# Talking-heads attention and a feed-forward block: the second batch's second mixing by three float16 products

## The chip, the cores and the metric

One core of a Trainium2 chip. The metric is device time in microseconds (us). Engines named here: TensorE (PE, with its weight loads as PEld), VectorE (DVE), ScalarE (ACT), GpSimd (POOL) and SyncE (SP), whose queue issues all DMAs.

## The reference

```
scores = einsum('bhij,hg->bgij', (q @ k^T) / 8, w_pre)       # first mixing, over 12 heads
attn   = exp(scores - max); attn = attn / (sum(attn) + 1e-9)
attn   = einsum('bhij,hg->bgij', attn, w_post)               # second mixing
x      = (attn @ v), as (1792 tokens, 768)
h = x @ w_in;  g = h * sigmoid(1.702 h);  out = g @ w_out    # 768 -> 2048 -> 768
```

There are 4 batches of 12 heads, 448 rows and 64 columns; everything comes in and goes out as float32.

## The kernel before

**Steps.** A batch's attention is done in 45 steps of 10 rows of the sequence (the last has 8). In a step the 10 rows and 12 heads are 120 partitions, and the 448 columns lie along the free axis, so that mixing the heads is one matrix product with a 120x120 matrix (`KG` = 120). There are 180 steps in all, numbered by `i`; steps 45 to 89 are the second batch (`b` = 1).

A step goes: `gather` (a DMA brings the scores `r`), `mix` (PE, first mixing into PSUM `mx`), `peak` (DVE, the row maximum), `expo` (ACT, the exponential `e` and its sum), `shifted` (POOL) and `inverse` (DVE), which make the factor `rs` of the normalization, and then the second mixing into PSUM `pp`, in one of two ways:

- **float32** (`whole`): `weigh_mix` (POOL) multiplies the 120x120 mixing matrix `wp` by `rs`, and `post_whole` (PE) multiplies the exponentials `e` with it: four chunks of 112 columns, one float32 product each, which the trace shows as two matmul instructions. `keep_whole` (ACT) copies `pp` to SBUF as one float32 array `p`.
- **float16**: `weigh` (POOL) makes `w` = `e` times `rs` in float32; `upper` (ACT) makes the same rounded to float16, `a1`; `lower` (POOL) subtracts the two to get the rest, `a2`, in float16. `post` (PE) adds three float16 products for each of the four chunks: `a1` with both parts of the mixing matrix (`wp1`, `wp2`) and `a2` with `wp1`. `keep_upper` (ACT) and `keep_lower` (DVE) store `pp` as two float16 parts.

The product of q and k (`scores`) and that with v (`context`) have the same two kinds: one float32 product, or three float16 products of two-part operands. In the kernel before, `WHOLE = 2` decides all of it: batches 0 and 1 go in float32, batches 2 and 3 by parts.

**Feed-forward.** The weights come as 32-bit halves of 64-bit numbers and are converted on the chip, in 16 conversions (8 slices of `w_in` and of `w_out`) of three parts each. A part takes on DVE `magnitude` (L473), `least` (L477), `shift` (L481), `rest` (L487), `sign` (L493) and, later, `w_lower` (L526), and on ACT a sum of squares and `w_upper`. The converted slices go to DRAM (`wd`) and come back as `wt` for each of 32 units (8 slices for each of 4 batches). A unit is 36 matmuls for h (`hidden`, L557), tanh and gating on ACT and DVE, and 36 matmuls for the output (`project`, L595).

**The order of the work.** The order on each engine is worked out when the program is built, by a greedy planner: `add` enters a task with its engines, an assumed duration, the tasks it comes after, a due time counted in steps and the buffers that it takes, and `run_all` picks among those that can start within 0.1 us the one that is due first. On the chip each engine then goes through its own list in that order. Conversions become due every 7 steps, then every 5, and their loads wait for the exponential of a given step (`gated_by`); the feed-forward's units follow at 12 pieces of work per 5.6 steps. The planner may put some copies and sums on either ACT or DVE. Buffers that matter here: `e` and `w` share three, `a1` and `wr` share three, `a2` has three, `mx` and `pp` have two PSUM banks each, and three banks serve the scores' products and the feed-forward.

Of the kernel before, what the change touches and what calls it, by code (L numbers as in the profile page):

```python
# [18 lines left out]

B, H, S, D = 4, 12, 448, 64  # L20
WHOLE = 2
DM, DFF = 768, 2048
NT = B * S
GI = 10
GPB = -(-S // GI)
GPC = 12
# [13 lines left out]
def attention_then_feed_forward(ctx, tc, q, k, v, w_pre, w_post, w_in, w_out, out):  # L40
    nc = tc.nc
# [14 lines left out]
    steps = [(b, g) for b in range(B) for g in range(GPB)]  # L56
# [9 lines left out]
    ex = keep.tile([128, B], F32, name="ex")  # L66
# [12 lines left out]
    def root_bits(e, m):  # L79

        nc.vector.tensor_scalar_max(m, m, 1e-30)
        nc.vector.tensor_scalar(
            e.bitcast(I32), m.bitcast(I32), 1, 0x7F800000,
            op0=ALU.logical_shift_right, op1=ALU.bitwise_and,
        )
# [55 lines left out]
    def top_of(name, b):  # L141
        i = 3 * b + "kqv".index(name)
        return tops[:, i:i + 1]

    def scale(name, b):

        m = top_of(name, b)
        e = stat.tile([128, 1], F32, name=f"e{name}_{b}", tag="e" + name)
        s = stat.tile([128, 1], F32, name=f"s_{name}{b}", tag="s" + name)
        root_bits(e, m)  # L150
        nc.vector.reciprocal(s, e)
        nc.vector.tensor_scalar_mul(s, s, 2.0 ** -50)
        nc.vector.tensor_scalar_mul(e, e, 2.0 ** 63)
        st["e" + name, b], st["s" + name, b] = e, s
        if name == "v":
            nc.vector.tensor_scalar(
                ex[:, b:b + 1], e, e_wp, 2.0 ** -12, op0=ALU.mult, op1=ALU.mult
            )
            if b < WHOLE:
                xs = st["xs", b] = keep.tile([128, 1], F32, name=f"xs_{b}")  # L160
                nc.vector.reciprocal(xs, ex[:, b:b + 1])

    def mixing(b):
        wa = keep.tile([KG, KG], F32, name=f"wa_{b}", tag="wa", bufs=2)
# [51 lines left out]
    def scores(b, c, pr, tag=("gen", 3)):  # L216
# [3 lines left out]
        w = NPAIR // THIRDS  # L220
        if b < WHOLE:
            qf, kf = st["q", b, pr // w], st["k", b, pr // w]
# [30 lines left out]
    def rows_of(g):  # L253
        return g * GI, min(GI, S - g * GI)
# [11 lines left out]
    def mix(i):  # L266
        b, g = steps[i]
        K = rows_of(g)[1] * H
        mx = ps.tile([128, 512], F32, name=f"mx_{i}", tag="mx", bufs=2)[:KG]
        row["mx", i] = mx  # L270
        nc.tensor.matmul(  # L271
            mx[:K, :S], st["wa", b][:K, :K], row.pop(("r", i))[:K, :], start=True, stop=True
        )

    def peak(i):
        K = rows_of(steps[i][1])[1] * H
        nm = stat.tile([KG, 1], F32, name=f"nm_{i}", tag="nm")
        nc.vector.tensor_reduce(nm[:K], row["mx", i][:K, :S], axis=AX.X, op=ALU.max, negate=True)  # L278
        row["nm", i] = nm

    def expo(i):
        K = rows_of(steps[i][1])[1] * H
        e = flow.tile([KG, S], F32, name=f"e_{i}", tag="e", bufs=3)
        sm = stat.tile([KG, 1], F32, name=f"sm_{i}", tag="sm")
        nc.scalar.activation(  # L285
            e[:K], row.pop(("mx", i))[:K, :S], AF.Exp, bias=row.pop(("nm", i))[:K, 0:1],
            scale=1.0, accum_out=sm[:K, 0:1],
        )
        row["e", i], row["sm", i] = e, sm

    def shifted(i):
        K = rows_of(steps[i][1])[1] * H
        sm = row.pop(("sm", i))
        rs = stat.tile([KG, 1], F32, name=f"rs_{i}", tag="rs")
        by = 1.0 if steps[i][0] < WHOLE else 2.0 ** -10
        nc.gpsimd.tensor_scalar(rs[:K], sm[:K], 1e-9, by, op0=ALU.add, op1=ALU.mult)  # L296
        row["rs", i] = rs

    def inverse(i):
        K = rows_of(steps[i][1])[1] * H  # L300
        nc.vector.reciprocal(row["rs", i][:K], row["rs", i][:K])  # L301
# [57 lines left out]
    def mixed_to(i):  # L359
        b, g = steps[i]  # L360
        n = rows_of(g)[1]
        c, off = g // GPC, (g % GPC) * GI
        if off == 0:
            shape, kind = ([CP, NR, H, CI], F32) if b < WHOLE else ([CP, 2, NR, H, CI], F16)
            st["p", b, c] = mixed.tile(shape, kind, name=f"p_{b}_{c}", tag="p")
        p = st["p", b, c]
        if b < WHOLE:
            return p.rearrange("p r h i -> p (r h) i")[:, :, off:off + n]
        return p.rearrange("p t r h i -> p t (r h) i")[:, :, :, off:off + n]
# [4 lines left out]
    def keep_upper(i):  # L374
        p = row["p", i] = mixed_to(i)
        nc.scalar.copy(p[:, 0], row["pp", i])  # L376

    def keep_lower(i):
        p = row.pop(("p", i))
        nc.vector.tensor_tensor(p[:, 1], row.pop(("pp", i)), p[:, 0], op=ALU.subtract)  # L380


    def context(b, c, pr):
# [5 lines left out]
        w = H // THIRDS  # L389
        if b < WHOLE:  # L390
            for jc in range(NR):
# [247 lines left out]
    def add(eng, occ, f, after=(), due=0.0, lat=None, size=0.0, takes=(), kind="", bias=0.0, behind=None):  # L639

        occ = occ if isinstance(occ, dict) else {e: occ for e in eng.split("/")}
        if lat is None:
            lat = {e: o + (0.2 if e == "PE" else 0.1) for e, o in occ.items()}
        lat = lat if isinstance(lat, dict) else {e: lat for e in occ}
        j = {"eng": tuple(occ), "occ": occ, "lat": lat, "f": f, "due": due, "size": size, "takes": list(takes),
             "kind": kind, "bias": bias, "left": 0, "then": [], "next": [], "at": None, "from": 0.0}
        for a in after:
            if a is not None:
                a["then"].append(j)
                j["left"] += 1  # L650
        if behind is not None:
            behind["next"].append(j)
            j["left"] += 1
        for x in j["takes"]:
            x[1].append(j)
        if not j["left"]:
            waiting.append(j)
        return j
# [207 lines left out]
    def step_tasks(i):  # L866

        b, g = steps[i]
        c, whole = g // GPC, b < WHOLE
        takes_p = [("p", p_home[b, c])] if g % GPC == 0 else []  # L870
        mx, pp = [], []
        m = mixes[i] = add("PE", 0.755, lambda: mix(i), [gathers.get(i), mixes.get(i - 1), mixers.get(b)], i - 1,
                           takes=[("mx", mx)])
        r_home[i].append(m)
        k = add("D", 0.53, lambda: peak(i), [m], i - 1, 0.62)
        early = expos.get(i, {"then": []})["then"]
        e = expos[i] = add("A", 0.62, lambda: expo(i), [k, expos.get(i - 1)], i - 0.8, 0.73, takes=[("e", e_home[i])])
        e["then"] += early
        mx += [k, e]
        r = add("G", 0.28, lambda: shifted(i), [e], i - 0.5, 0.26)  # L880
        v = add("D", 0.08, lambda: inverse(i), [r], i - 0.5, 0.16)

        def emit_post():
            (post_whole if whole else post)(i)
            last_pp_home.append(pp)

        if whole:
            wr = []
            w = add("G", 0.45, lambda: weigh_mix(i), [v], i, 0.4, takes=[("a1", wr)])
            p = add("PE", 0.84, emit_post, [w, e, posts.get(i - 1)], i + 1, takes=[("pp", pp)])  # L890
            wr.append(p)
            e_home[i].append(p)
            q = add("A", 0.45, lambda: keep_whole(i), [p], i + 2, 0.58, takes=takes_p)
            pp.append(q)
        else:
            w_home, a1, a2 = [], [], []
            w = add("G", 0.72, lambda: weigh(i), [v], i, 0.7, takes=[("e", w_home)])
            u = add("A", 0.56, lambda: upper(i), [v], i + 0.3, 0.66, takes=[("a1", a1)])
            lo = add("G", 1.12, lambda: lower(i), [w, u], i + 0.6, 1.05, takes=[("a2", a2)])
            e_home[i] += [w, u]  # L900
            w_home.append(lo)
            p = add("PE", 0.64, emit_post, [lo, u, posts.get(i - 1)], i + 2, takes=[("pp", pp)])
            a1 += [lo, p]
            a2.append(p)
            h = add("A", 0.45, lambda: keep_upper(i), [p], i + 2.8, 0.56, takes=takes_p)
            q = add("D", 0.56, lambda: keep_lower(i), [h], i + 3.2, 0.65)
            pp += [h, q]
        posts[i], keeps[i] = p, q
        p_home[b, c].append(q)
        if not first_post:  # L910
            first_post.append(p)
# [138 lines left out]
    for i in range(N):  # L1050
        if i + AHEAD < N:
            b, g = steps[i + AHEAD]
# [24 lines left out]
        b, g = steps[i]  # L1077
# [18 lines left out]
    for u in range(NU):  # L1096
        s, b = units[u]
# [6 lines left out]
        for fc in range(SF):  # L1104
            gen, th = [], []
            j = None
            for x in range(3):
                due = due_of["h", u, fc, x] - 1.5 * (x > 0)
                j = add("PE", 1.134, lambda u=u, fc=fc, x=x: hidden(u, fc, x), [got[0, u], x_done[b], j], due,
                        takes=[] if x else [("gen", gen)], kind="ff")  # L1110
# [15 lines left out]
        for e in range(NCC):  # L1126
# [6 lines left out]
            takes = [("acc", acc_home[b])] if (s, e) == (0, 0) else [("pt", pt, "A")] if 0 < s < NS - 1 else []  # L1133
# [60 lines left out]
```

## Time and profile before

| | |
|---|---|
| median of 3 runs | 928.07 us (927.72 to 929.06) |
| the profiled execution's own time | 930.12 us |
| its span, first to last instruction | 928.4 us |
| matmul instructions | 6972 |
| busy over the span: PE, DVE, ACT, POOL | 97%, 63%, 64%, 36% |
| mean granted TensorE clock | 0.992 of full speed |

Busy time of an engine counts a moment once, even where two of its instructions overlap; TensorE's matmuls overlap in the trace, where their ends are modelled, so the rate of TensorE is read from start to start. The "chain of waits" follows the work that ended last back in time, at each step to what released it. A stretch is given in us from the start of the span.

### The profile page before, as it was taken

How to read it: one execution, taken by the hardware profiler on the slowest of the kernel's cores; microseconds unless marked ns; L12 is line 12 of the kernel's file. 1: busy time of each engine (PE TensorE's matmuls, PEld its weight loads, DVE VectorE, ACT ScalarE, POOL GpSimd, SP SyncE). 2: the span in 40 equal slices, each digit the busy share in tenths (PEclk: the TensorE clock that was granted, in tenths of full speed). 3: DMA queues.
4: the chain of work that ended last, by engine and by line, in shares of the span. 5: the costliest groups of instructions: out<-in, count | busy, mean ns of one | idle time of the engine just before them, and what ended most of it. 6: DMA issues, size and time to landing. Idle time of an engine off the chain costs nothing.

```text
span 928.4 us, 18998 instructions
## 1 busy us (share of the span) xinstructions
PE 897.2 (97%) x6972; PEld 535.5 (58%) x6972; DVE 589.4 (63%) x1342; ACT 593.3 (64%) x1328; POOL 337.8 (36%) x532
## 2 busy tenths in 40 slices
PE   7879989999999999989999999999999999999998
PEld 5455656656566566655656555555656666545554
DVE  2678787687789978977567656567555554332233
ACT  2668787697875776765696776666675665324342
POOL 0212222221225313546346744455344553203431
PEclk9999999999999999999999999999999999999999
DMA  7878999997988796669576575567443422343322
GB/s 235 288 257 298 321 305 329 320 314 230 335 294 287 231 299 207 204 194 328 168 249 221 162 238 162 164 176 255 140 154 111 129 99 83 123 133 132 136 75 88
DMA packets 66256, 196.76 MB, mean 212 GB/s; under 512 B 7699, under 2 KB 32403, under 8 KB 66163
## 3 DMA queue, kind: packets, MB, share of 16 engines
q1 hardware_dynamic: 66162, 195.54, 65.1%
q8 instruction: 55, 0.90, 0.4%
q14 instruction: 39, 0.31, 0.1%
HBM read 138.89 MB, written 56.62 MB: 211 GB/s over the span
## 4 chain that ended last, share of the span: by engine, by line
PE 75%; DVE 9%; DMA 6%; ACT 5%; issue 2%; POOL 2%; SPq 1%; ACTq 0%; POOLq 0%; DVEq 0%
PE po L595 20%; PE h L557 20%; PE mx L271 12%; PE pp L316 5%; PE av L394 3%; PE av L405 3%; PE qk L225 3%; PE qk L235 3%; DMA r<-sd 2%; PE pp L353 2%; PE pp L355 2%; PE pp L354 2%; DVE nm L278 2%; ACT e L285 1%; ACT waste L96 1%
## 5 line engine op out<-in xcount | busy, mean ns | idle before, releaser
L557 PE MATMUL h<-x,wt 128*128 128x448 f16 x1152 | 246.8, 352 | 3.2 <-DMA wt<-wd 2.9
L595 PE MATMUL po<-g,wt 128*128 128x448 f16 x1152 | 239.7, 352 | 4.3 <-DVE th L576 2.4
L271 PE MATMUL mx<-r,wa 120*120 120x448 f32 x360 | 172.3, 563 | 5.2 <-DMA r<-sd 3.1
L557 PEld LDWEIGHTS <-wt 128*128 128x128 f16 x1152 | 109.2, 98 | 115.5 <-issue 26.4
L285 ACT ACTIVATE e<-mx,nm 120x448 f32<-120x448 f32 x180 | 113.9, 633 | 96.4 <-DVE nm L278 84.5
L595 PEld LDWEIGHTS <-wt 128*128 128x128 f16 x1152 | 109.9, 98 | 108.4 <-issue 16.7
L296 POOL TENSOR_SCALAR rs<-sm 120x1 f32<-120x1 f32 x180 | 46.8, 260 | 336.6 <-ACT e L285 333.3
L278 DVE TENSOR_REDUCE nm<-mx 120x1 f32<-120x448 f32 x180 | 111.4, 619 | 46.3 <-PE mx L271 44.9
L623 POOL TENSOR_TENSOR acc<-acc,pt 128x448 f32<-128x448 f32 x64 | 72.8, 1138 | 117.3 <-ACT pt L617 116.9
L316 PEld LDWEIGHTS pp<-wr,e 120*112 120x112 f32 x720 | 84.4, 177 | 40.9 <-issue 18.9
L576 DVE SCALAR_TENSOR_TENSOR th<-th,h 128x448 f32<-128x448 f32 x64 | 39.6, 619 | 105.9 <-ACT th L572 105.5
L340 POOL TENSOR_TENSOR a<-w,a 120x448 f16<-120x448 f32 (+1 forms) x90 | 95.8, 1064 | 26.3 <-POOL w L326 17.6
L316 PE MATMUL pp<-wr,e 120*112 120x120 f32 x720 | 91.4, 270 | 6.0 <-POOL wr L306 6.0
L246 ACT COPY sc<-qk 120x448 f32<-120x448 f32 (+1 forms) x150 | 74.5, 532 | 15.7 <-PE qk L225 11.3
L619 DVE SCALAR_TENSOR_TENSOR acc<-po,ct,acc 128x448 f32<-128x448 f32 x104 | 70.3, 679 | 22.0 <-PE po L595 21.1
L271 PEld LDWEIGHTS mx<-r,wa 120*120 120x120 f32 x360 | 57.8, 184 | 37.4 <-issue 16.2
L326 POOL TENSOR_SCALAR w<-e,rs 120x448 f32<-120x448 f32 (+1 forms) x90 | 60.5, 672 | 40.8 <-DVE rs L301 35.0
L617 ACT ACTIVATE pt<-po,ct 128x448 f32<-128x448 f32 x64 | 40.6, 634 | 51.1 <-PE po L595 51.0
L334 ACT ACTIVATE a<-e,rs 120x448 f16<-120x448 f32 (+1 forms) x90 | 60.3, 670 | 18.4 <-DVE rs L301 17.2
L380 DVE TENSOR_TENSOR p<-pp,p 112x480 f16<-112x480 f32 (+1 forms) x90 | 58.4, 649 | 19.2 <-ACT p L376 18.9
L306 POOL TENSOR_SCALAR wr<-wp,rs 120x120 f32<-120x120 f32 (+1 forms) x90 | 47.4, 527 | 54.0 <-DVE rs L301 33.7
L353 PE MATMUL pp<-wp,a 120*112 120x120 f16 x360 | 62.3, 217 | 0.0
(123 smaller groups left out, 1323.0 us busy)
## 6 DMA issues: line engine op xcount, KB each, us to landing
wt<-wd SPq DMA_DIRECT2D x64, 768.0 KB
r<-sd SPq DMA_DIRECT2D x176, 210.0 KB
sd<-sc SPq DMA_DIRECT2D x66, 420.0 KB
w<-in_moe_w_in_dram SPq DMA_DIRECT2D x24, 512.0 KB
w<-in_moe_w_out_dram SPq DMA_DIRECT2D x24, 512.0 KB
wd<-w_p SPq DMA_DIRECT2D x16, 768.0 KB
sd<-sc SPq DMA_DIRECT2D x24, 308.0 KB
out_dram<-acc SPq DMA_DIRECT2D x24, 224.0 KB
```

The source lines that it names most:

```text
L246: (nc.scalar.copy if eng == "A" else nc.vector.tensor_copy)(t[:n, x, :], two[x][:n, :S])
L271: nc.tensor.matmul(mx[:K, :S], st["wa", b][:K, :K], row.pop(("r", i))[:K, :], start=True, stop=True)
L278: nc.vector.tensor_reduce(nm[:K], row["mx", i][:K, :S], axis=AX.X, op=ALU.max, negate=True)
L285: nc.scalar.activation(e[:K], row.pop(("mx", i))[:K, :S], AF.Exp, bias=row.pop(("nm", i))[:K, 0:1], scale=1.0, accum_out=sm[:K, 0:1],)
L316: nc.tensor.matmul(pp[:CP, jc * K:(jc + 1) * K], e[:K, jc * CP:(jc + 1) * CP], wr[:K, :, :n], start=True, stop=True,)
L326: nc.gpsimd.tensor_scalar(w[:K], e[:K], row["rs", i][:K, 0:1], 1.0, op0=ALU.mult, op1=ALU.mult)
L340: nc.gpsimd.tensor_tensor(a2[:K], row.pop(("w", i))[:K], row["a1", i][:K], op=ALU.subtract)
L353: nc.tensor.matmul(o, a1[:K, js], wp1[:K, :, :n], start=True, stop=False)
L557: nc.tensor.matmul(h, w[:, i, c, fc * 128:(fc + 1) * 128], x[:, j, c, :], start=(n == 0), stop=(n == len(terms) - 1),)
L595: nc.tensor.matmul(po, w[:, j, fc, e * 128:(e + 1) * 128], g[:, i, fc, :], start=(n == 0), stop=(n == len(terms) - 1),)
L619: nc.vector.scalar_tensor_tensor(a, po, c, a, op0=ALU.mult, op1=ALU.add)
L623: nc.gpsimd.tensor_tensor(a, a, st.pop(("pt", u, e)), op=ALU.add)
```

## The change

A second bound, `EXACT = 1`, decides about the second mixing; `WHOLE = 2` still decides about the products with k and with v. So batch 1 takes `weigh`, `upper`, `lower` and `post`, and then `keep_whole`: one float32 copy of `pp`, and the float32 product with v. The factor `rs` of batch 1 gets the 2^-10 of the float16 way, and the scale `xs` that the output of the attention is multiplied by follows from that.

```diff
+EXACT = 1
 ...
             if b < WHOLE:
                 xs = st["xs", b] = keep.tile([128, 1], F32, name=f"xs_{b}")
-                nc.vector.reciprocal(xs, ex[:, b:b + 1])
+                if b < EXACT:
+                    nc.vector.reciprocal(xs, ex[:, b:b + 1])
+                else:
+                    nc.vector.tensor_scalar_mul(xs, s, 2.0 ** -15)
 ...
-        by = 1.0 if steps[i][0] < WHOLE else 2.0 ** -10
+        by = 1.0 if steps[i][0] < EXACT else 2.0 ** -10
 ...
-        c, whole = g // GPC, b < WHOLE
+        c, whole = g // GPC, b < EXACT
 ...
-            h = add("A", 0.45, lambda: keep_upper(i), [p], i + 2.8, 0.56, takes=takes_p)
-            q = add("D", 0.56, lambda: keep_lower(i), [h], i + 3.2, 0.65)
-            pp += [h, q]
+            h = add("A", 0.45, lambda: (keep_whole if b < WHOLE else keep_upper)(i), [p], i + 2.8, 0.56, takes=takes_p)
+            q = h if b < WHOLE else add("D", 0.56, lambda: keep_lower(i), [h], i + 3.2, 0.65)
+            pp += [h] if b < WHOLE else [h, q]
```

## Rows read from the trace of the kernel before

**Rows 1.** The profile's page, busy time of each engine over the span.
```profile
span 928.4 us, 18998 instructions
PE 897.2 (97%) x6972; PEld 535.5 (58%) x6972; DVE 589.4 (63%) x1342; ACT 593.3 (64%) x1328; POOL 337.8 (36%) x532
```

**Rows 2.** The page's chain of work that ended last, by engine and by line.
```profile
PE 75%; DVE 9%; DMA 6%; ACT 5%; issue 2%; POOL 2%; SPq 1%; ACTq 0%; POOLq 0%; DVEq 0%
PE po L595 20%; PE h L557 20%; PE mx L271 12%; PE pp L316 5%; PE av L394 3%; PE av L405 3%; PE qk L225 3%; PE qk L235 3%; DMA r<-sd 2%; PE pp L353 2%; PE pp L355 2%; PE pp L354 2%; DVE nm L278 2%; ACT e L285 1%; ACT waste L96 1%
```

**Rows 3.** Stretches: length; busy us (instructions) per engine; granted clock, DMA share, GB/s.
```profile
160.00:365.00 205.00, 201.50 (x1392) 125.40 (x1393) 167.78 (x413) 150.72 (x364) 55.93 (x103) 0.99 0.86 281
180.00:200.00 20.00, 19.88 (x113) 11.80 (x112) 17.99 (x48) 18.11 (x47) 6.07 (x14) 1.00 1.01 308
280.00:320.00 40.00, 37.82 (x250) 23.46 (x249) 38.00 (x78) 24.86 (x57) 17.02 (x22) 1.00 0.78 255
365.00:412.00 47.00, 44.12 (x375) 26.56 (x372) 39.67 (x89) 31.73 (x71) 21.69 (x29) 1.00 0.66 206
425.00:765.00 340.00, 339.09 (x3123) 201.49 (x3122) 204.57 (x430) 230.54 (x502) 170.58 (x249) 1.00 0.58 182
```

**Rows 4.** Stretches of the float32 second mixing's matmuls alone (L316): PE, PEld.
```profile
160.00:368.00 208.00, 44.93 (x360) 42.84 (x360) 0.99 0.86 282
```

**Rows 5.** Timeline of PE, batch 1: start, duration, instructions.
```profile
263.14 0.92 PE L271 MATMUL mx<-r,wa 120*120 120x448 f32 x2
263.90 0.98 PE L316 MATMUL pp<-wr,e 120*112 120x120 f32 x8
264.72 1.30 PE L557 MATMUL h<-x,wt 128*128 128x448 f16 x6
```

**Rows 6.** Timeline of PE, batch 2: a step's first and last float16 product.
```profile
570.80 0.22 PE L353 MATMUL pp<-wp,a 120*112 120x120 f16 x1
...
571.38 0.22 PE L355 MATMUL pp<-wp,a 120*112 120x120 f16 x1
571.43 0.73 PE L557 MATMUL h<-x,wt 128*128 128x448 f16 x3
```

**Rows 7.** The page's groups: count, busy us, mean ns, idle before and its releaser.
```profile
L340 POOL TENSOR_TENSOR a<-w,a 120x448 f16<-120x448 f32 (+1 forms) x90 | 95.8, 1064 | 26.3 <-POOL w L326 17.6
L326 POOL TENSOR_SCALAR w<-e,rs 120x448 f32<-120x448 f32 (+1 forms) x90 | 60.5, 672 | 40.8 <-DVE rs L301 35.0
L334 ACT ACTIVATE a<-e,rs 120x448 f16<-120x448 f32 (+1 forms) x90 | 60.3, 670 | 18.4 <-DVE rs L301 17.2
L306 POOL TENSOR_SCALAR wr<-wp,rs 120x120 f32<-120x120 f32 (+1 forms) x90 | 47.4, 527 | 54.0 <-DVE rs L301 33.7
```

**Rows 8.** Groups on DVE in 160 to 365, three of the conversion's lines.
```profile
L487 DVE SCALAR_TENSOR_TENSOR w_f<-w,w_f 128x512 int32<-128x512 int32 x26 | 18.4, 707 | 0.4
L526 DVE SCALAR_TENSOR_TENSOR w_p<-w_f,w_s,w_p 128x512 f16<-128x512 f32 x24 | 17.3, 746 | 1.1 <-ACT w_p L521 0.9
L477 DVE TENSOR_SCALAR w_f<-w_f 128x512 f32<-128x512 f32 x26 | 11.7, 449 | 0.3
```

**Rows 9.** The same lines on DVE in 365 to 412.
```profile
L526 DVE SCALAR_TENSOR_TENSOR w_p<-w_f,w_s,w_p 128x512 f16<-128x512 f32 x6 | 5.1, 871 | 0.0
L487 DVE SCALAR_TENSOR_TENSOR w_f<-w,w_f 128x512 int32<-128x512 int32 x3 | 3.1, 1033 | 0.1
L477 DVE TENSOR_SCALAR w_f<-w_f 128x512 f32<-128x512 f32 x3 | 3.0, 1009 | 0.0
```

**Rows 10.** Timeline of all engines at 391 to 397.
```profile
391.43 1.08 POOL L340 TENSOR_TENSOR a<-w,a 120x448 f16<-120x448 f32 x1
...
391.66 1.40 DVE L487 SCALAR_TENSOR_TENSOR w_f<-w,w_f 128x512 int32<-128x512 int32 x1
...
397.05 0.74 PE L557 MATMUL h<-x,wt 128*128 128x448 f16 x3 [2.88 <-DMA wt<-wd]
```

## The prediction

> **What bounds the kernel now.** I read the page's busy times first, then its chain of waits, then a table of stretches, and last the timeline of single steps. The busy times say TensorE: 97% of the span, with DVE and ACT at 63% and 64% [rows 1]. The reader is to check that this isn't only a long tail of overlapping matmuls, and the chain of waits does that: 75% of the time that led to the end is PE's own work, and the float32 second mixing (L316) alone is 5% of it [rows 2]. But the mean hides the stage that matters. Batch 1's 45 second mixings, 8 matmul instructions each, lie between 160 and 368 us [rows 4], and in 160 to 365 DVE is busy 167.8 of 205 us (82%) and ACT 150.7 (74%), against 60% and 68% in 425 to 765 [rows 3]. The conversions of the weights run in that stage too, 26 parts of them [rows 8]. So TensorE is the bound there, at 201.5 of 205 us, but with two engines not far behind it.
>
> **What the change does on TensorE.** A float32 mixing starts at 263.90 and the next matmul at 264.72, that is 0.82 us a step [rows 5]. By three float16 products it is 12 matmuls from 570.80 to the next product at 571.43, 0.63 us [rows 6]; both are followed by the same kind of matmul. So 0.19 us goes from each step, times 45 is 8.55 us of TensorE's work, all of it in a stage where TensorE has 3.5 us of idle time in 205. Nothing else on TensorE changes: the products with k and v stay float32.
>
> **What it adds elsewhere.** ACT gets `upper`, 45 x 0.670 = 30.2 us [rows 7]; `keep_whole` stays. POOL loses `weigh_mix`, 45 x 0.527 = 23.7, and gets `weigh` and `lower`, 45 x (0.672 + 1.064) = 78.1 [rows 7], a net 54.4. DVE gets no instruction: `inverse` stays, `keep_lower` isn't used, and the scale `xs` is one small multiplication in place of one reciprocal, once in the program, which I cost at nothing because it lies in the work of sizing v, many steps before the first use. POOL goes from 55.9 to about 110 us of 205, which is the share that it has in 425 to 765 (170.6 of 340) with PE busy 339.1 of 340 [rows 3]: POOL by itself isn't the bound. ACT goes from 150.7 to about 181 us, or 90% of a stage of 201 us. No DMA is added or moved past another in its due time.
>
> The new path is also longer. In float32 the post waits for a POOL instruction of 0.527 us after the reciprocal; now it waits for 0.672 + 1.064 = 1.74 us of POOL, or 1.2 us more [rows 7]. The post becomes due one step later (i + 2 in place of i + 1), and a step of this stage takes 205/45 = 4.6 us, so I cost the latency at nothing: the feed-forward's matmuls and the next `mix` cover it. If that cover is gone, it costs 1.2 us at the four ends of a chunk where `context` waits for the last copy, 5 us in all, and that is within the range below. The buffers `e`, now shared with `w`, were shared in batches 2 and 3 already, at 340 us for 75 steps (4.5 us each), with PE idle for 0.9 us [rows 3].
>
> **What of the 8.55 us is left.** That depends on how much TensorE idles once ACT, DVE and POOL are fuller. The trace has no stretch with all three as full as they will be, so I bound the idle share by the nearest three [rows 3]. At 180 to 200, ACT is at 91% and DVE at 90%, and PE idles 0.12 of 20 us (0.6%). At 280 to 320, DVE is at 95%, and PE idles 2.18 of 40 (5.5%). At 365 to 412 the very mix of the changed kernel is seen, float16 steps beside conversions, and PE idles 2.88 of 47 (6.1%), which is one wait for a converted weight tile [rows 10]. TensorE's work in the stage becomes 201.5 - 8.55 = 192.95 us. At 0.6% idle the stage lasts 194.1 us (10.9 less than now), at 6.1% it lasts 205.5 (0.5 more). I take the mean of the three, 4.1%, since the first has the fullness and the last the mix: 192.95/0.959 = 201.2 us, 3.8 less than now. Before 160 and after 412 the work is unchanged, and from 425 to 765 TensorE idles for 0.9 us [rows 3], so that what is won is kept and what is lost isn't made up.
>
> The durations are from an execution of 930.12 us with a span of 928.4; it would come to 926.3. The median of the runs is 2.05 us below it, and so I forecast 928.07 - 3.8 = 924.3 us.
>
> **The rivals.**
>
> *Full gain (917.2 us).* The planner moves copies from ACT to DVE and back as they fill, and the idle share is that of 180 to 200: 10.9 us less. For it: the fullest stretch of the two engines has the least idle time [rows 3]. Against: it is only 20 us long.
>
> *VectorE becomes the bound (933 us, slower).* In 365 to 412, where POOL does float16 steps, the conversion's DVE instructions are longer than in 160 to 365, where it doesn't: L477 1009 ns against 449, L487 1033 against 707, L526 871 against 746 [rows 8, 9]. That is 0.560 + 0.326 + 0.125 = 1.01 us for each part of a conversion. The timeline shows how: L487, started 0.23 us after POOL's L340, takes 1.40 us in place of 0.7 and ends 0.55 us after it [rows 10], so it looks as if it had waited for POOL's instruction to end. The 26 parts of 160 to 365 would so cost DVE 26.3 us more, 194.1 in all. At the share that DVE reaches in its two fullest stretches, 95% and 90% [rows 3], 92.5% between them, the stage lasts 209.8 us, 4.8 more than now: 933 us (204 to 216 us of stage by the two shares, 927.4 to 938.8 us). It decides from the point where DVE at 90% needs more than 205 us, which is 16.7 us of added work or 0.64 us a part; the planner has no such cost and can't evade it. Against it: the means of L477 and L487 in 365 to 412 come from three instructions each.
> The Trainium skill (SBUF — State Buffer, section "Who interferes with whom") says that VectorE and GpSimd share one pair of ports under an exclusive lock: a VectorE instruction with two SBUF inputs, or in a two-port mode, and a GpSimd instruction that reads SBUF block each other for a whole instruction, whichever started first. By that rule L477, L487 and L526 would all be exposed, which the longer means agree with, and the time would be this rival's.
>
> *The wait for weights eats it (928 us).* At 394 TensorE waits 2.88 us for a converted tile [rows 10]. If the conversions don't come earlier, TensorE arrives up to 8.55 us sooner and waits that much longer. Against it: their loads are gated by the exponentials of given steps, which come earlier as well; DVE has to keep pace.
>
> *The change doesn't do what it says*: the float16 products being no faster. The 90 steps of batches 2 and 3 already have them, so I give it nothing.
>
> **How the numbers follow.** A measurement of this kernel can tell 0.2%, 1.9 us, from no change: 926.2 to 929.9 us. My forecast's case, 921 to 926.2, gets 0.41; full gain, below 921, gets 0.15; the wait for weights, within 0.2%, gets 0.17; VectorE as the bound, above 929.9, gets 0.27. So faster 0.56, same 0.17, slower 0.27. Cases of both signs hold much of the chance; the likeliest one's own range is 921 to 926.2. The range that should hold the time 8 times in 10 reaches from the full gain to just above the slower rival's 933: 917 to 935, which leaves out some 0.05 below and 0.13 above.
>
> **What would show it.** Right: batch 1's `pp` takes 12 matmuls in 0.63 us; ACT's 30 us and POOL's 54 us are added between 160 and 360; the last second mixing of batch 1 starts about 4 us earlier and everything after it by as much; PE's idle time in the stage rises from 3.5 to about 8 us. Wrong towards slower: L477, L487 and L526 in that stage near their 365 to 412 means, DVE over 90%, and PE waiting for DVE or for `wt`. Wrong towards faster: PE's idle time no larger than now. What would make it wrong altogether is another order of work after 412 that leaves TensorE idle where it now isn't, since the planner works the whole order out anew.

## The result and the profile after

The changed kernel takes 941.20 us (median of 6 runs, 938.96 to 945.77) against 929.32 us for the kernel before (6 runs, 927.72 to 930.67): a ratio of 1.0130, with a 95% interval of 1.0102 to 1.0158. It is slower, where 3.8 us less were forecast. The ratios, here and below, are taken against runs of the kernel before that were measured beside each kernel; they differ from the quotient of the two medians by up to 0.2%. The profiled execution has a span of 940.2 us.

The page of the changed kernel, busy times and the chain of waits (its lines are numbered 4 higher from the step functions on; L316 is now L320, L353 to L355 are L357 to L359):

```profile
span 940.2 us, 19441 instructions
PE 893.8 (95%) x7152; PEld 527.5 (56%) x7152; DVE 615.0 (65%) x1345; ACT 615.6 (65%) x1369; POOL 405.3 (43%) x582
PE 56%; DVE 15%; ACT 2%; DMA 1%; issue 1%; POOL 1%; SPq 0%; ACTq 0%; POOLq 0%
```

Against [rows 1] PE is busy 3.4 us less in a span that is 11.8 us longer, and DVE, to which the change itself gives no instruction (the planner moved three there), is busy 25.6 us more. The chain's shares add up to 77% here (it couldn't be followed back further) and to 100% in [rows 2], so that PE's fall from 75% to 56% says little by itself; but DVE's share rises from 9% to 15% in spite of it. In 220 to 430, which both chains cover, DVE has 43 of the 210 us before and 121 after, PE 119 and 46, POOL 7 and 6. The stretches, with the columns of [rows 3], say where:

```profile
160.00:375.00 215.00, 195.59 (x1544) 115.53 (x1546) 189.78 (x411) 168.68 (x398) 118.76 (x148) 0.98 0.81 264
280.00:320.00 40.00, 32.06 (x243) 18.95 (x241) 39.61 (x64) 24.67 (x54) 29.42 (x30) 0.91 0.75 243
430.00:780.00 350.00, 349.63 (x3257) 208.64 (x3257) 214.35 (x444) 239.88 (x519) 179.18 (x257) 1.00 0.59 184
```

All of it is in batch 1's stage: from the first mixing of step 45 to that of step 110, 294.6 us became 307.0, and the 12.4 us are lost before step 90. In 160 to 375 TensorE idles 215 - 195.6 = 19.4 us (9.0%), against 3.5 of 205 before [rows 3]; from 430 to 780 it idles 0.4 us, so it is busy there as it was. The float16 mixing itself does what it should, 12 matmuls from 186.95 to 187.58, 0.63 us (timeline of PE):

```profile
186.95 0.22 PE L357 MATMUL pp<-wp,a 120*112 120x120 f16 x1
...
187.53 0.22 PE L359 MATMUL pp<-wp,a 120*112 120x120 f16 x1
187.58 0.97 PE L275 MATMUL mx<-r,wa 120*120 120x448 f32 x2
```

DVE's groups in 160 to 376 show the conversion's six lines. Where the same line is in [rows 8], the mean was 707 (now L491), 746 (L530) and 449 ns (L481). The other three before (now L497, L477 and L485), in 160 to 365, and then all six after:

```profile
L493 DVE SCALAR_TENSOR_TENSOR w_f<-w,w_f 128x512 int32<-128x512 int32 x25 | 19.1, 764 | 0.2
L473 DVE TENSOR_SCALAR w_f<-w 128x512 int32<-128x512 int32 x26 | 11.3, 433 | 3.2 <-DMA w<-in_moe_w_in_dram 2.3 <-DMA w<-in_moe_w_out_dram 0.8
L481 DVE TENSOR_SCALAR w_f<-w_f 128x512 int32<-128x512 int32 x26 | 11.0, 425 | 0.4
```

```profile
L491 DVE SCALAR_TENSOR_TENSOR w_f<-w,w_f 128x512 int32<-128x512 int32 x25 | 23.0, 923 | 0.2
L497 DVE SCALAR_TENSOR_TENSOR w_f<-w,w_f 128x512 int32<-128x512 int32 x25 | 20.3, 814 | 0.3
L530 DVE SCALAR_TENSOR_TENSOR w_p<-w_f,w_s,w_p 128x512 f16<-128x512 f32 x25 | 19.9, 820 | 0.5 <-ACT w_p L525 0.5
L485 DVE TENSOR_SCALAR w_f<-w_f 128x512 int32<-128x512 int32 x25 | 15.2, 611 | 0.3
L477 DVE TENSOR_SCALAR w_f<-w 128x512 int32<-128x512 int32 x26 | 14.4, 553 | 0.5 <-DMA w<-in_moe_w_in_dram 0.5
L481 DVE TENSOR_SCALAR w_f<-w_f 128x512 f32<-128x512 f32 x25 | 13.5, 544 | 0.3
```

The timeline of all engines at the largest wait shows how a longer DVE instruction becomes idle time of TensorE:

```profile
307.65 1.38 POOL L627 TENSOR_TENSOR acc<-acc,pt 128x448 f32<-128x448 f32 x1
308.08 1.24 DVE L481 TENSOR_SCALAR w_f<-w_f 128x512 f32<-128x512 f32 x1
...
309.45 1.20 POOL L201 TENSOR_SCALAR qp<-qb,s_q 128x896 f16<-128x896 f32 x1
309.81 1.38 DVE L491 SCALAR_TENSOR_TENSOR w_f<-w,w_f 128x512 int32<-128x512 int32 x1
310.62 1.46 POOL L344 TENSOR_TENSOR a<-w,a 120x448 f16<-120x448 f32 x1
311.23 1.40 DVE L497 SCALAR_TENSOR_TENSOR w_f<-w,w_f 128x512 int32<-128x512 int32 x1
...
312.72 0.63 ACT L97 ACTIVATE waste<-w_f 128x512 bf16<-128x512 f32 x1 [0.69 <-DVE w_f L497]
...
313.35 0.55 ACT L376 COPY p<-pp 112x480 f32<-112x480 f32 x1
313.95 0.59 PE L109 MATMUL pp<-w_m,ones 128*128 128x3 f32 x2 [7.14 <-ACT p L376]
```

L491 starts while POOL's L201 runs and ends 0.54 us after it; L497 starts while `lower` (L344) runs and ends 0.55 us after that. In 160 to 378, 16 of the 50 `rest` and `sign` instructions took longer than 0.72 us; all 16 had started inside an instruction of POOL, and they ended 0.534 to 0.552 us after it. The 14 of the 50 `least` and `shift` that took longer than 0.46 us had also started inside one, and ended 0.279 to 0.287 us after it. So a DVE instruction that is held up goes on when POOL's is over, and not before. (Not every one that starts inside a POOL instruction is held up: an L481 at 301.19 takes its usual 0.42 us, and there POOL's L330 takes 0.99 us in place of 0.64. POOL's own instructions are stretched as well, L330 up to 1.21 us; by what isn't shown.) ACT's sum of squares (L97) then waits for L497, the copy of `pp` (L376) stands behind it in ACT's list, and TensorE's small matmul that adds up the squares (L109) waits for both; it is next in TensorE's list, and nothing behind it may start for 7.14 us. During this wait, at 310.3 us, TensorE's granted clock falls to its lower level, 1.2 GHz, and stays there to 317.2 us.

### The profile page after: what moved, and what is told of

It is laid out like the page before. It is cut to its first block, busy times and chain, and to the rows that moved or that the text cites. A ratio compares the mean times of both kernels' runs of the same rounds, so it can differ in the third digit from the quotient of the medians.

```text
span 940.2 us, 19441 instructions
## 1 busy us (share of the span) xinstructions
PE 893.8 (95%) x7152; PEld 527.5 (56%) x7152; DVE 615.0 (65%) x1345; ACT 615.6 (65%) x1369; POOL 405.3 (43%) x582
## 4 chain that ended last, share of the span: by engine, by line
PE 56%; DVE 15%; ACT 2%; DMA 1%; issue 1%; POOL 1%; SPq 0%; ACTq 0%; POOLq 0%
PE po L599 18%; PE h L561 18%; PE mx L275 7%; PE av L409 3%; PE qk L239 3%; PE pp L357 2%; PE pp L359 2%; PE pp L358 2%; DVE w_f L497 2%; DVE w_f L491 2%; DVE w_p L530 1%; DVE nm L282 1%; DVE w_f L485 1%; DVE w_f L477 1%; DVE acc L623 1%
## 5 line engine op out<-in xcount | busy, mean ns | idle before, releaser
L599 PE MATMUL po<-g,wt 128*128 128x448 f16 x1152 | 242.2, 353 | 6.9 <-DVE th L580 2.9
L300 POOL TENSOR_SCALAR rs<-sm 120x1 f32<-120x1 f32 x180 | 47.4, 263 | 282.2 <-ACT e L289 275.9
L344 POOL TENSOR_TENSOR a<-w,a 120x448 f16<-120x448 f32 x135 | 145.2, 1076 | 45.8 <-POOL w L330 23.6
L627 POOL TENSOR_TENSOR acc<-acc,pt 128x448 f32<-128x448 f32 x68 | 78.6, 1157 | 108.3 <-ACT pt L621 108.0
L330 POOL TENSOR_SCALAR w<-e,rs 120x448 f32<-120x448 f32 x135 | 97.2, 720 | 58.6 <-DVE rs L305 46.3
L338 ACT ACTIVATE a<-e,rs 120x448 f16<-120x448 f32 x135 | 90.3, 670 | 28.2 <-DVE rs L305 26.7
L359 PE MATMUL pp<-wp,a 120*112 120x120 f16 x540 | 93.2, 216 | 2.0 <-POOL a L344 2.0
L357 PE MATMUL pp<-wp,a 120*112 120x120 f16 x540 | 93.6, 216 | 0.3 <-ACT p L376 0.3
L358 PE MATMUL pp<-wp,a 120*112 120x120 f16 x540 | 93.1, 216 | 0.0
L275 PEld LDWEIGHTS mx<-r,wa 120*120 120x120 f32 x360 | 58.5, 185 | 43.2 <-issue 19.4
L358 PEld LDWEIGHTS <-a 120*112 120x112 f16 x540 | 70.2, 130 | 22.3 <-issue 19.5
L623 DVE SCALAR_TENSOR_TENSOR acc<-po,ct,acc 128x448 f32<-128x448 f32 x100 | 67.9, 679 | 22.0 <-PE po L599 21.4
L357 PEld LDWEIGHTS <-a 120*112 120x112 f16 x540 | 70.1, 130 | 20.6 <-issue 13.0
L621 ACT ACTIVATE pt<-po,ct 128x448 f32<-128x448 f32 x68 | 42.9, 634 | 51.0 <-PE po L599 50.8
```

The source lines that it names most:

```text
L275: nc.tensor.matmul(mx[:K, :S], st["wa", b][:K, :K], row.pop(("r", i))[:K, :], start=True, stop=True)
L330: nc.gpsimd.tensor_scalar(w[:K], e[:K], row["rs", i][:K, 0:1], 1.0, op0=ALU.mult, op1=ALU.mult)
L338: nc.scalar.activation(a1[:K], row["e", i][:K], AF.Copy, scale=row["rs", i][:K, 0:1])
L344: nc.gpsimd.tensor_tensor(a2[:K], row.pop(("w", i))[:K], row["a1", i][:K], op=ALU.subtract)
L357: nc.tensor.matmul(o, a1[:K, js], wp1[:K, :, :n], start=True, stop=False)
L358: nc.tensor.matmul(o, a1[:K, js], wp2[:K, :, :n], start=False, stop=False)
```

## The experiments

Theory A: POOL's long instructions hold up DVE's. Theory B: ACT's 30 us fill it up. Theory C: the longer way from exponential to post. Theory D: the newly planned order is a bad one. The first four kernels keep the order of a parent's instructions; the traces of the first two have the changed kernel's sequence of instructions on PE, DVE, ACT and POOL. Those two, `m1_write_only` and `m3_half` leave the rest `a2` out of batch 1's result, so that they price a cause and can't be used as kernels.

**POOL's two instructions cut to 8 columns** (`s1_narrow`).

```diff
+        m = 8 if steps[i][0] == 1 else S
-            w[:K], e[:K], row["rs", i][:K, 0:1], 1.0, op0=ALU.mult, op1=ALU.mult
+            w[:K, :m], e[:K, :m], row["rs", i][:K, 0:1], 1.0, op0=ALU.mult, op1=ALU.mult
...
-            a2[:K], row.pop(("w", i))[:K], row["a1", i][:K], op=ALU.subtract
+            a2[:K, :m], row.pop(("w", i))[:K, :m], row["a1", i][:K, :m], op=ALU.subtract
...
+        if steps[i][0] == 1:
+            a2 = a1
```

> The changed kernel in its own order of work, with batch 1's two POOL instructions cut to 8 of 448 columns, and its third product taken from a1 (so the rest a2 is left out of batch 1's result and no matmul waits for POOL). TensorE, ACT and DVE have the same instructions in the same order. Theory A (POOL's long instructions hold up DVE's conversion instructions): the conversion's six DVE lines fall back to their means of the kernel before (about 430 to 760 ns), DVE's busy time in the stage falls by some 20 us, and the time falls from 941 to 920-928 us. Theory B (ACT's added 30 us fill it up): 938-943, since ACT keeps them. Theory C (the longer way from the exponential to the post): falls as well, to 920-930. Theory D (the newly planned order is a bad one, whatever the durations): 936-943 with DVE's lines short.

925.25 us (4 runs), 0.9926 of before (0.9900 to 0.9952). DVE's lines in 160 to 376 (three of the six):

```profile
L534 DVE SCALAR_TENSOR_TENSOR w_p<-w_f,w_s,w_p 128x512 f16<-128x512 f32 x26 | 19.3, 771 | 0.8 <-ACT w_p L529 0.4
L495 DVE SCALAR_TENSOR_TENSOR w_f<-w,w_f 128x512 int32<-128x512 int32 x27 | 19.7, 734 | 0.3
L485 DVE TENSOR_SCALAR w_f<-w_f 128x512 f32<-128x512 f32 x27 | 12.2, 453 | 0.3
```

They are back near [rows 8]. With ACT's 30 us, the same order and TensorE's saving, the kernel is 0.74% faster than before by the ratio, some 6.9 us (5.4 us by the medians, 930.68 and 925.25; in its trace steps 45 to 110 take 291.0 us, 3.6 less than before). B and D fall as main causes; A and C stand. TensorE's small matmul (L109) still waits once for 3.9 us, so that not all of the 7.14 us is due to these two instructions.

**POOL's instructions whole, nobody waits for them** (`s2_unread`): only `a2 = a1` in `post`.

> The changed kernel in its own order of work, POOL's two instructions whole, but batch 1's third product taken from a1, so that no matmul waits for POOL's result (the rest a2 is left out of batch 1's result). Theory A (POOL's instructions hold up DVE's): DVE's conversion lines stay long (550 to 920 ns) and the time stays at 936-941 us. Theory B (ACT full): 938-943. Theory C (latency of the new way): 920-930. Theory D (the order): 936-943.

940.92 us, 1.0097 (1.0068 to 1.0127). Taking TensorE's wait for POOL away gains 0.3 us by the medians and some 3 by the ratios, whose intervals overlap, so C falls as a main cause. Between this and the run above nothing differs but the width of POOL's instructions: 15.7 us. ACT's instructions are as long in both (`upper` 667 and 670 ns); DVE is busy for 260.6 us from step 45 to step 110, and for 240.0 with 8 columns.

A rival for these 15.7 us is POOL's own queue: with the wide instructions, the small one that makes `rs` (L300) starts 0.49 us after the exponential's sum, on average over batch 1, and 0.12 us with 8 columns. The chain of waits speaks against it: of the 210 us in 220 to 430, POOL has 7.5 here and 3.2 with 8 columns, DVE 108.7 and 60.7.

**The kernel before with the same work on POOL** (`s3_before_pool`), placed in `weigh_mix`:

```diff
+            nc.gpsimd.tensor_scalar(x1[:K], e[:K], rs[:K, 0:1], 1.0, op0=ALU.mult, op1=ALU.mult)
+            nc.gpsimd.tensor_tensor(x2[:K], e[:K], x1[:K], op=ALU.subtract)
```

> The kernel before in its own order, with two more POOL instructions per step of batch 1 behind weigh_mix, of the size of weigh and lower (120x448), whose results nobody reads; a new wr then comes up to 1.7 us later if POOL still works on them. Theory A: DVE's conversion lines get as long as in the changed kernel (550 to 920 ns in place of 430 to 760), DVE's busy time in the stage rises by 20 us or more, and the time from 929 to 940-955 us (no saving on TensorE here). Theory B (ACT), theory C (latency of the new way) and theory D (the new order): 928-932, DVE's lines unchanged.

957.24 us, 1.0278 (1.0250 to 1.0305): 26.6 us slower, above what I gave. DVE's groups in 160 to 390, and then TensorE's longest waits in it:

```profile
L533 DVE SCALAR_TENSOR_TENSOR w_p<-w_f,w_s,w_p 128x512 f16<-128x512 f32 x26 | 22.0, 870 | 0.5 <-ACT w_p L528 0.2
L494 DVE SCALAR_TENSOR_TENSOR w_f<-w,w_f 128x512 int32<-128x512 int32 x25 | 20.6, 824 | 0.4
L484 DVE TENSOR_SCALAR w_f<-w_f 128x512 f32<-128x512 f32 x26 | 13.4, 515 | 0.3
```

```profile
PE pp L323 <- POOL wr L306: 7.5, 7, 1.7
PE pp L108 <- ACT p L379: 6.8, 2, 3.8
```

The float32 kernel gets the long DVE lines too, and the same wait at the small sum. 7.5 us of it are the experiment's own, the matmuls that wait for a `wr` queued behind the added work, and so it isn't a clean price.

**The kernel before with the same work on ACT** (`s4_before_act`), `upper`'s activation placed in the same spot.

> The kernel before in its own order, with one more ACT instruction per step of batch 1, the one that makes a1 (120x448 to float16), whose result nobody reads. Theory B (ACT's 30 us are what costs): ACT at 90% in the stage, time 936-945 us. Theories A, C and D: 928-933 us, since TensorE still bounds the stage and ACT had 26% idle.

934.97 us (10 runs), 1.0043 (1.0023 to 1.0063). ACT's 30 us aren't free, as A had it, but cost 4 us in this order and not 12.

**POOL writes and reads nothing** (`m1_write_only`):

```diff
+            for _ in range(2):
+                nc.gpsimd.memset(w[:K], 1.0)
...
+            for _ in range(2):
+                nc.gpsimd.memset(a2[:K], 1.0)
```

> As the run with POOL's results unread (940.9 us), but POOL fills the two tiles with a constant, twice each, in place of computing them: it writes and reads nothing (the rest a2 is left out of batch 1's result). If POOL's reading of SBUF is what holds DVE up in every line: all six conversion lines short (430 to 760 ns), 921-928 us. If POOL's write is enough for the one-input lines (L473, L477, L481 of the kernel before) and its read is needed for the two-input ones (L487, L493, L526): the first three long (over 500 ns), the other three short (under 780 ns), 928-936 us. If any long POOL instruction does it: all six long, 937-943 us. How long such a fill takes no trace of this case shows; POOL's busy time will tell how far the dose is the same.

926.89 us (10 runs), 0.9963 (0.9944 to 0.9982). POOL is busy with the fills for 92 us, more than the 86 of `weigh` and `lower` in `s2_unread`, in pieces of half a microsecond. So POOL's being busy isn't by itself what costs; but `rs` starts 0.25 us after the sum here, between the two runs above, so that a part for POOL's queue isn't wholly ruled out. POOL's two groups, and DVE's six, in 160 to 376:

```profile
L350 POOL MEMSET a<- 120x448 f16 (+1 forms) x90 | 46.5, 517 | 3.7
L332 POOL MEMSET w<- 120x448 f32 (+1 forms) x90 | 45.5, 506 | 4.2 <-ACT a L342 0.5
```

```profile
L507 DVE SCALAR_TENSOR_TENSOR w_f<-w,w_f 128x512 int32<-128x512 int32 x27 | 20.7, 766 | 0.3
L501 DVE SCALAR_TENSOR_TENSOR w_f<-w,w_f 128x512 int32<-128x512 int32 x27 | 20.7, 768 | 0.3
L540 DVE SCALAR_TENSOR_TENSOR w_p<-w_f,w_s,w_p 128x512 f16<-128x512 f32 x24 | 18.0, 773 | 0.7 <-ACT w_p L535 0.4
L495 DVE TENSOR_SCALAR w_f<-w_f 128x512 int32<-128x512 int32 x28 | 15.4, 554 | 0.4
L491 DVE TENSOR_SCALAR w_f<-w_f 128x512 f32<-128x512 f32 x28 | 14.8, 530 | 0.3
L487 DVE TENSOR_SCALAR w_f<-w 128x512 int32<-128x512 int32 x28 | 14.5, 517 | 1.2 <-DMA w<-in_moe_w_in_dram 1.2
```

The instructions with one input are still long, those with two inputs in SBUF are short (734 to 771 ns in the run with 8 columns). So the two kinds are held up by different things: those with two inputs aren't held up by a POOL instruction that only writes, those with one input are. The lines are those of the second expectation, the time that of the first. The fills are shorter than `weigh` and `lower` (0.51 us against 0.79 and 1.14), so that the price of the writing alone, and how much of the 15.7 us is the reading, isn't settled.

**Half the dose** (`m3_half`): `weigh` cut to 8 columns, `lower` whole.

> As the run with POOL's results unread (940.9 us), with weigh cut to 8 of 448 columns and lower whole (it reads a1 twice; the rest a2 is left out of batch 1's result). Some 48 of POOL's 78 us stay. If the cost is in proportion to POOL's time, 61% of the 15.7 us between 925.25 and 940.9 stays: 933-937 us. If DVE has slack that takes up the first part of it, 925-930 us.

931.77 us (10 runs), 1.0024 (1.0008 to 1.0041). 61% of POOL's time leaves 6.5 of the 15.7 us by the medians, 42%, and 57% by the ratios: between the two expectations, and a cost in proportion isn't ruled out.

**The planner told** (`m2_planner_told`): the same instructions, other assumed durations.

```diff
+        slow = 38 <= first < 92
...
+                occ += (0.11, 0.10, 0.18, 0.24, 0.13)[n] * slow
```

That is for the conversion's five lines; `w_lower` gets 0.1 us more, the lower parts of batch 2's q and k 0.5, `weigh` of batch 1 0.16.

> The changed kernel, with the planner told the longer durations: the conversion's five DVE lines and w_lower by 0.10 to 0.24 us more in batch 1, q's and k's lower parts of batch 2 by 0.5, weigh by 0.16. Every instruction is the same, only the order is planned anew. If the loss comes from lists that were made for shorter DVE instructions (TensorE's 7.1 us wait for a sum is of that kind): 926-934 us. If DVE's capacity itself is what is missing, 936-943 us.

928.66 us (10 runs), 0.9975 (0.9954 to 0.9997): the changed kernel, with only its order planned anew, is no longer slower than before. The stretch 160 to 375, and two of DVE's lines in 160 to 376:

```profile
160.00:375.00 215.00, 206.44 (x1613) 120.73 (x1612) 196.71 (x425) 179.21 (x422) 129.69 (x157) 0.99 0.85 272
```

```profile
L491 DVE SCALAR_TENSOR_TENSOR w_f<-w,w_f 128x512 int32<-128x512 int32 x26 | 22.1, 865 | 0.0
L481 DVE TENSOR_SCALAR w_f<-w_f 128x512 f32<-128x512 f32 x26 | 18.4, 716 | 0.1
```

Four of DVE's six conversion lines are longer than in the changed kernel and two are shorter (L491 with 865 against 923 ns, L477 with 454 against 553), and DVE is busier; yet TensorE idles 8.6 us in place of 19.4. What the hold-ups cost depends on whether the lists leave room for them.

**Only the sums later** (`c3_sum_later`): the squares of batch 1's conversions assumed 4 us later.

> The changed kernel, with the planner told only that the conversions' sums of squares are there 4 us later in batch 1, so that TensorE's small matmul over them stands later in its list; all durations of DVE as planned before. If the loss is mainly TensorE standing at that one matmul (9.7 us of its waits in the stage): 929-934 us. If it is spread over every list that waits for DVE: 936-942 us.

935.93 us (7 runs), 1.0054 (1.0030 to 1.0079). By the ratios this gives back some 7 of the 12 us, between the two expectations. The trace shows less: the small matmul's waits in 160 to 376 fall from 9.7 to 2.3 us, but steps 45 to 110 take 304.0 us against 307.0, since TensorE now waits elsewhere. The order of the work also differs in other places, from 181 us on. So that wait was the largest single one, 9.7 of 19.4 us, and what it cost by itself, 3 to 7 us, stays open.

**The control** (`c1_before_told`): the kernel before with the same durations told.

> The control for the run with the planner told: the kernel before, float32 second mixing in batch 1, with the same longer durations told to the planner (they are wrong here, since its DVE lines are short). If telling the planner is worth something by itself: 924-928 us. If it only repairs what POOL's float16 work does to DVE: 929-935 us, the same as before or a little slower, since DVE's room is planned and not used.

925.68 us (6 runs), 0.9937 (0.9912 to 0.9961). The first expectation holds: the room is worth 0.6% (0.5% by the medians) to the float32 kernel as well. Its stretch of 365 to 412, where [rows 3] had TensorE idle for 2.88 us and [rows 10] show the wait for a weight tile:

```profile
365.00:412.00 47.00, 47.00 (x397) 28.09 (x396) 40.46 (x90) 35.11 (x80) 29.12 (x33) 1.00 0.75 231
```

With the planner told in both, the changed kernel has 0.9975 and the kernel before 0.9937. That points to the change being worth nothing in a good order either, but the intervals overlap between 0.9954 and 0.9961, and so the sign of this small difference isn't settled.

**Float32 for 12 steps more** (`f_chunk_more`): batch 2's first chunk takes `weigh_mix` and `post_whole`, with the mixing matrix scaled as the float16 way has it.

> The kernel before with the float32 second mixing kept for the 12 steps of batch 2's first chunk too, where conversions still run (to 412 us): TensorE gets 12 x 0.19 = 2.3 us more, POOL loses 12 x 1.21 = 14.5 us, ACT 12 x 0.67 = 8 us. If POOL's instructions beside conversions are what costs, the conversion lines in 365 to 412 fall back to 430 to 760 ns (about 1 us a part, 6 parts, and some 1.5 us of v's splits), and the time is 924-929 us against 929 to 930; if not, TensorE's 2.3 us show: 931-933 us.

926.13 us (9 runs), 0.9953 (0.9932 to 0.9974): the change run backwards, at the only other place where float16 steps stand beside conversions, is a gain, though TensorE has 2.3 us more to do. In its trace 3.0 us are won from step 92 on, where its order first differs from that of the kernel before (but for one instruction at the start, which scales the matrix), about the 2.88 us of [rows 10]. ACT's busy time is nearly the same there (31.59 us, 31.73 in [rows 3]), DVE's is 4.8 us less. The stretch, and three of DVE's lines in it, against [rows 9] (871, 1033 and 1009 ns):

```profile
365.00:412.00 47.00, 47.00 (x352) 29.85 (x351) 34.91 (x85) 31.59 (x70) 16.28 (x26) 1.00 0.68 212
```

```profile
L528 DVE SCALAR_TENSOR_TENSOR w_p<-w_f,w_s,w_p 128x512 f16<-128x512 f32 x6 | 4.4, 742 | 0.1
L489 DVE SCALAR_TENSOR_TENSOR w_f<-w,w_f 128x512 int32<-128x512 int32 x3 | 2.6, 865 | 0.1
L479 DVE TENSOR_SCALAR w_f<-w_f 128x512 f32<-128x512 f32 x3 | 1.3, 421 | 0.0
```

**Combinations.** The changed kernel, planner told, with the float32 chunk (`c2_told_chunk`), and the kernel before with both (`c4_chunk_told`):

> The changed kernel with the planner told (0.9975 of before) and the float32 second mixing in the 12 steps of batch 2's first chunk (0.9953 of before by itself). If the two gains come from different stages and add up: 0.992 to 0.994 of before, 923-926 us. If they are the same gain (the same conversions coming sooner): 0.995 to 0.998, 926-929 us.

926.79 us (7 runs), 0.9950 (0.9924 to 0.9975).

> The two versions that were faster than the kernel before, together: float32 second mixing in batch 1 and in batch 2's first chunk (0.9953 of before) and the planner told longer DVE durations (0.9937). If the planner's gain is room around the conversions of 365 to 412, which the float32 chunk has already freed: 0.993 to 0.996. If they are separate gains: 0.989 to 0.991, 919-921 us.

926.55 us (12 runs), 0.9950 (0.9929 to 0.9972). The gains don't add up. Both single versions leave TensorE no idle time in 365 to 412, so much of it is the same 2.88 us won twice; that this is all of it isn't shown.

## Why the prediction was wrong

**What held.** TensorE bounds the kernel, the float16 mixing takes 0.63 us in place of 0.82, and with POOL out of the way the kernel gains between 3.6 (in the trace) and 6.9 us (by the ratio) in `s1_narrow`, of the 8.55 that I had worked out. The latency of the new way costs next to nothing (`s2_unread`). Behind the stage nothing is lost: what follows the first mixing of step 110 takes 1.0 us less than before.

**The step that failed** is the one on what is left of the 8.55 us. I took TensorE's idle share as 4.1%, the mean of three stretches of the kernel before; it is 9.0%. The sum left DVE's instructions as long as they were, and so put POOL's hold-up of DVE at nothing; DVE was busy 189.8 us in the stage in place of 167.8. The stretch at 180 to 200, by which a full DVE and ACT hardly cost TensorE anything, had POOL busy for 6.1 of 20 us, so it said nothing on the case at hand. And the stretch at 365 to 412 did contain the cause, but I read its idle time as one number, 2.88 us, and set its longer DVE lines aside as a rival's.

**The rival with VectorE as the bound** is what happened, in place and in the hold-up, though not with DVE's capacity as the bound. Its price was 933 us. The hold-up of its three lines is smaller than I had it: for L477, L487 and L526 together (544 - 449) + (923 - 707) + (820 - 746) = 385 ns and not 1.01 us; the means of [rows 9] came from three to six instructions. The other three lines, which the price left out, are held up as well, by (814 - 764) + (553 - 433) + (611 - 425) = 356 ns. So it is partly luck that DVE's 189.8 us in the stage are near the rival's 194.1. But the stage is 10 us longer all the same, because DVE reached a share of 88% (189.8 of 215) and not 92.5%. That is what I had left out: the lists of all engines were fixed for the short durations, so one late DVE instruction stops ACT's and TensorE's lists too (7.14 us at one small matmul, of which `s1_narrow` keeps 3.9). With room planned for it, DVE gets to 91% (196.7 of 215) and the loss is gone (`m2_planner_told`). So the cost is, in the main, POOL's hold-up of DVE: 15.7 us or 1.7% by the width of its instructions alone. Some 0.9% of it came through lists without room: 1.0130 - 0.9975 is 1.55%, less the 0.63% that the room is worth without POOL's work (`c1_before_told`); each ratio is known to about 0.25%, so that this share is rough.

The Trainium skill (SBUF — State Buffer, section "Who interferes with whom") says that VectorE and GpSimd lock their shared ports for a whole instruction, and that a two-input VectorE instruction contends with a GpSimd instruction that reads SBUF and not with one that only writes it. The traces agree: the fixed offset to POOL's end (0.53 to 0.55 and 0.28 to 0.29 us), and 766 to 773 ns for the two-input lines beside 92 us of fills.

**The other rivals.** The full gain (917.2 us) isn't reached even with POOL out of the way (925.25). The wait for weights wasn't what ate the gain: TensorE's idle time rose in 160 to 375, and most of it at sums and copies. ACT, which I held harmless at 90%, costs 4 us by itself (`s4_before_act`).

## What to carry to other kernels

Work moved to an idle engine is not free if its instructions hold up another engine's: look in the trace for the same instruction at two lengths, and at which instruction of the other engine its end is tied to, before taking busy shares as room. In a program with fixed lists, a stretch whose instructions get longer than the planner assumed can lose time though no engine is full (DVE at 88% here), above all at the small matmuls that join several engines. Telling the planner the measured durations is the cheap repair (1.0130 became 0.9975); the same room was worth 0.6% in the unchanged kernel too (`c1_before_told`), the best ratio of the kernels here that compute the whole result, with an interval that overlaps those of the other faster ones.

## What was not expected of the hardware

POOL's fills of half a microsecond, 180 of them, lengthened the one-input DVE lines to 517 to 554 ns (446 to 472 with 8 columns) and left the two-input ones as they were. And in TensorE's 7.14 us of waiting, 306.8 to 313.95, the granted clock fell to its lower level for 6.8 us, 310.3 to 317.2, while the 2.88 us wait before the change [rows 10] brought no fall (clock 1.00 in 365 to 412, [rows 3]). The length of a wait alone doesn't decide it: in `c3_sum_later` the clock fell at 306.4, at the end of a wait of 2.33 us.
